# A revised hand-written order for windowed attention followed by a gated convolution: the output projection one group behind the value projection, block-sum trees ahead of their transposes, normalisation in its own step, v in 4096-byte rows, w_out earlier

## The chip, the cores and the metric

The kernel runs on one core of one Trainium2 chip. A core has a matrix engine (PE in the profile; its weight loads are shown as PEld), a vector engine (DVE), a scalar engine (ACT), a general engine (POOL), and a queue engine (SP) that issues the transfers between HBM and the on-chip memory. Each engine works through its own instructions in the order in which they were written, and waits on semaphores for the others. The metric is the device time of one execution in microseconds; lower is better.

## The reference

Inputs are q, k and v of shape (4 batches, 8 heads, 768 positions, 64 dims), and the weights w_val (512 x 512), conv_w (5 x 512) and w_out (512 x 512). What is computed, cut to the core:

```
k_sum = k.reshape(B, H, 24, 32, D).max(axis=3)
v_sum = v.reshape(B, H, 24, 32, D).mean(axis=3)
scores = concat([where(|i-j| < 16, q k^T / 8, -1e9), q k_sum^T / 8 + log(32)])
a      = softmax(scores)
x      = a @ concat([v, v_sum])            # heads side by side: (B, 768, 512)
gate   = sigmoid(causal 5-tap depthwise convolution of x with conv_w)
out    = (gate * (x @ w_val)) @ w_out
```

Each query so sees a window of 31 neighbours and the 24 block summaries of its head.

## The kernel before

**Tiles.** A *unit* (b, th, hp) is a third of a batch's positions (256, four query tiles of 64) for four heads (two pairs of heads, pr). There are 24 units, numbered in order; two units (hp = 0 and 1) make a *group* of 256 positions with all 512 channels, and there are 12 groups (g). Three groups are a batch.

**What one unit goes through.**
- mm_s (line 310): scores on PE into a PSUM tile with one buffer; snorm (line 327): eight DVE instructions that scale, add the mask and take the row minimum of the negated scores.
- exps (line 341): eight exponentials on ACT with their row sums.
- norm (lines 349, 350, 353): two small DVE instructions make the reciprocal ri of the sums; two POOL multiplications apply it to p.
- tp (line 366): two times four PE transposes of p; pcopy (line 370): ACT copies them to SBUF as pts.
- mm_x (line 386): 32 matmuls of pts with v. Besides the window's rows, the v tile holds the batch's block sums, put there by fill_vs (line 187).
- xout (lines 401 to 404): ACT writes x rounded (xh) and in full (xf); POOL takes the difference, xl.
- ginit, taps (lines 416, 427, 431): the convolution, five taps for each of two pairs. The first tap is ACT's in groups below ACT_TAP_G and DVE's from there on; the other four are DVE's.
- gate (line 439): tanh on ACT.

**What one group goes through.** val (line 456) for each half of the channels (cp): 24 matmuls on xh and xl. val_ev (lines 466 to 468): gf = (gate + 1) * val on DVE, its rounded form gh on ACT, the difference gl on POOL. out (line 480) for each half of the positions (si): 12 matmuls on gh and gl of the whole group; out_ev (lines 487, 488): a copy on ACT and the store. Group 0 uses unsplit weights in val. w_val and w_out arrive as 64-bit words; conv_w (lines 200 to 203) turns a quarter of one into float32 with an ACT and two DVE instructions, split_w (lines 240, 241) makes the rounded part on ACT and the rest on POOL. The raw quarters of w_out lie in the buffers of xh and xl, and the staged float32 quarters of w_out have two buffers.

**Per batch.** load_k, load_vT and prep_k (lines 119, 129; DVE: block maxima into the k tile), prep_v (line 140; POOL: block sums as a tree of five adds) and prep_vs (lines 175, 177; PE transposes of the four sums, ACT copy), followed by fill_vs. LOAD_K, PREP_K and PREP_V say how many steps before the batch's first unit these stand.

**The order** is written out by hand, and the program keeps it on each engine. After a prologue for units 0 to 3 comes step(s) for s from 4 to 25 (line 531). A step holds different stages of three units: scores and exponentials of unit s, transposes of unit s-1, mm_x, xout and convolution of unit s-2. Two places in a step, at its start and between the two transposes of unit s-1, call proj(), which takes the next entry from a queue of projections. queue_proj adds val, val, out, out of a group at the end of the step in which the group's second x and gate were made, an odd step. So the step after it runs the two val and the next one the two out. norm(s-1) stands at the start of step s.

Of the kernel before, what the change touches and what calls it, by code (L numbers as in the profile page):

```python
# [35 lines left out]
KALLOC = OFF_A + 2 * STEP * (NT // 2 + 1)  # L36
NK = 5
HALO = NK - 1
REBIAS = 2.0 ** ((127 - 1023) // 8)
NHP = NPR // 2  # L40
NP = 2 * TPU
ACT_TAP_G = 5
LOADS = "k0 q0 m k1 q1 n0 i k2 q2 n1 k3 q3 n2 n3 v0 c Q w0 w1 w2 w3 v1 o0 o1 o2 o3"
LOAD_K = (-4, -3, -2, -1)
PREP_K = (-2, -1, -1, 0)
PREP_V = (-3, -2, -1, 0)


@with_exitstack
def tile_attention_then_gated_conv(  # L50
# [56 lines left out]
    def load_v(g):  # L107
        b, th = divmod(g, NTH)
        t = ld.tile([KW, TPU, DM], F32, tag="v", name=f"v_{g}")
        pieces = ((0, WIN), (OFF_O, OFF_B), (OFF_N, KW)) if g > 1 else ((0, KW),)  # L110
        for r0, r1 in pieces:
            nc.sync.dma_start(t[r0:r1], vw[b, th, r0:r1])
        vtile[g] = t

    def prep_k(b, pr):
# [230 lines left out]
    def norm(u):  # L346
        s = st[u]
        ri = wk.tile([P, NP], F32, tag="ri", name=f"ri_{u}", bufs=4)
        nc.vector.tensor_scalar(ri, s["rs"], 1e-9, None, ALU.add)
        nc.vector.reciprocal(ri, ri)  # L350
        for r in range(2):
            w = slice(TPU * r, TPU * r + TPU)
            nc.gpsimd.tensor_tensor(  # L353
                s["p"][:, w],
                s["p"][:, w],
                ri[:, w].unsqueeze(2).broadcast_to([P, TPU, KW]),
                ALU.mult,
            )
# [49 lines left out]
    def ginit(u):  # L408
        b, th, hp = units[u]
        g = b * NTH + th  # L410
        s = st[u]
        xp = s["xp"]
        gt = s["gt"] = ps_g.tile([P, 2, SG], F32, tag="g", name=f"g_{u}")
        if g < ACT_TAP_G:
            for r in range(2):
                nc.scalar.activation(
                    gt[:, r], xp[:, r], AF.Copy, scale=cwt[:, 2 * hp + r, NK - 1 : NK]
                )

    def taps(u):  # L420
        b, th, hp = units[u]
        g = b * NTH + th
        gt, x = st[u]["gt"], group(g)["xf"]
        for r in range(2):
            pr = 2 * hp + r
            if g >= ACT_TAP_G:
                nc.vector.tensor_scalar(  # L427
                    gt[:, r], x[:, pr, HALO:], cwt[:, pr, NK - 1 : NK], None, ALU.mult
                )
            for o in range(NK - 1):  # L430
                nc.vector.scalar_tensor_tensor(  # L431
                    gt[:, r], x[:, pr, o : o + SG], cwt[:, pr, o : o + 1], gt[:, r],
                    ALU.mult, ALU.add,
                )
# [58 lines left out]
    def proj():  # L493
        if not queue:
            return lambda: None
        mm, ev, g, i = queue.pop(0)
        pp = mm(g, i)
        return lambda: ev(g, i, pp)

    def queue_proj(g):  # L500
        queue.extend((val_mm, val_ev, g, cp) for cp in range(NHP))
        queue.extend((out_mm, out_ev, g, si) for si in range(SG // P))

    def early_loads(s):
        g, hp = divmod(s, NHP)
        if hp == 0 and 1 <= g < NG - 1:
            load_q(g + 1)
        for b in range(1, B):
            for i in range(NPR):
                if s - b * NTH * NHP == LOAD_K[i]:  # L510
                    load_k(b, i)
                    load_vT(b, i)

    def late_loads(s):
        g, hp = divmod(s, NHP)
        for b in range(1, B):
            w = s - b * NTH * NHP
            for i in range(NPR):
                if w == PREP_K[i]:
                    prep_k(b, i)  # L520
                if w == PREP_V[i]:
                    prep_v(b, i)
            if w == 0:
                prep_vs(b)
                fill_vs(b * NTH)
        if hp == NHP - 1 and 1 <= g < NG - 1:
            load_v(g + 1)
            if (g + 1) % NTH:
                fill_vs(g + 1)

    def step(s, late=lambda: None):
        if s < NU:
            early_loads(s)
        if 4 <= s - 1 < NU:
            norm(s - 1)
        ev = proj()
        if s - 2 < NU:
            mm_x(s - 2)
        ev()
        if s - 2 < NU:  # L540
            xout(s - 2)
            ginit(s - 2)
        if s < NU:
            mm_s(s, 0)
            mm_s(s, 1)
            snorm(s, 0)
            snorm(s, 1)
        if s - 1 < NU:
            tp(s - 1, 0)
        if s < NU:  # L550
            exps(s, 0)
        if s - 1 < NU:
            pcopy(s - 1, 0)
        if s < NU:
            exps(s, 1)
        if s - 2 < NU:
            taps(s - 2)
        ev = proj()
        if s - 1 < NU:
            tp(s - 1, 1)  # L560
            pcopy(s - 1, 1)
        ev()
        if s - 2 < NU:
            gate(s - 2)
            if units[s - 2][2] == NHP - 1 and s > 3:
                queue_proj((s - 2) // NHP)
        late()
        if s < NU:
            late_loads(s)

    prep_k(0, 0)
# [37 lines left out]
    mm_s(2, 1)
    snorm(2, 0)  # L610
    snorm(2, 1)
    mm_x(1)
    xout(1)
    conv_w("wv", 1)
    split_w("wv", 0)
    conv_w("wv", 2)
    exps(2, 0)
    split_w("wv", 1)
    conv_w("wv", 3)
    exps(2, 1)  # L620
    early_loads(2)
    mm_s(3, 0)
    mm_s(3, 1)
    ppv = [val_mm(0, 0)]
    taps(0)
    gate(0)
    ginit(1)
    norm(2)
    snorm(3, 0)
    snorm(3, 1)  # L630
    exps(3, 0)
    tp(2, 0)
    pcopy(2, 0)
    val_ev(0, 0, ppv[0])
    exps(3, 1)
    split_w("wv", 2)
    ppv.append(val_mm(0, 1))
    taps(1)
    gate(1)
    tp(2, 1)  # L640
    pcopy(2, 1)
    early_loads(3)
    norm(3)
    val_ev(0, 1, ppv[1])
    split_w("wv", 3)
    conv_w("wo", 0)
    split_w("wo", 0)
    late_loads(3)

    def late4():  # L650
        for k in range(1, 4):
            conv_w("wo", k)
            split_w("wo", k)
        queue.extend((out_mm, out_ev, 0, si) for si in range(SG // P))

    step(4, late4)
    for s in range(5, NU + 2):
        step(s)
    while queue:
        proj()()  # L660
# [6 lines left out]
def _layout(q, k, v, moe_w_val, moe_conv_w, moe_w_out):  # L667
    f = np.float32
    qT = q.reshape(B, NPR, 2, NTH, SG, D).transpose(0, 3, 2, 5, 1, 4)
    qT = qT.reshape(B, NTH, 2 * D, NPR, SG)  # L670
    kt = k.reshape(B, NPR, 2, S, D).transpose(0, 1, 2, 4, 3).reshape(B, NPR, 2 * D, S)
    kT = np.zeros((B, NPR, 2 * D, KTOT), f)
    for t in range(NT):
        c = OFF_O + STEP * t
        kT[..., c : c + QT] = kt[..., t * QT : (t + 1) * QT]
    vT = v.reshape(B, NPR, 2, S, D).transpose(0, 1, 2, 4, 3).reshape(B, NPR, 2 * D, S)
    vn = np.zeros((B, S + 2 * WIN, DM), f)
    vn[:, WIN : WIN + S] = v.transpose(0, 2, 1, 3).reshape(B, S, DM)
    vw = np.zeros((B, NTH, KW, TPU, DM), f)
    for t in range(NT):  # L680
        for r0, r1, s0 in ((0, WIN, 0), (OFF_O, OFF_B, WIN), (OFF_N, KW, WIN + QT)):
            n0 = t * QT + s0
            vw[:, t // TPU, r0:r1, t % TPU] = vn[:, n0 : n0 + r1 - r0]
    cw = moe_conv_w.reshape(NK, NPR, 2 * D).transpose(2, 1, 0).reshape(2 * D, NPR * NK)

    def words(a):
        a = np.ascontiguousarray(a)
        return a.view(np.int64) if a.dtype == np.float64 else a

    loc = np.full(KW, -1)  # L690
    loc[:WIN] = np.arange(WIN)
    loc[OFF_O:OFF_B] = WIN + np.arange(QT)
    loc[OFF_N:] = WIN + QT + np.arange(WIN)
    qi = np.arange(2 * D)[:, None] % QT
    second = np.arange(2 * D)[:, None] >= QT
    maskc = np.zeros((2 * D, 3, KW), f)
    for mv in range(3):
        lo = np.where((mv == 0) & ~second, WIN, 0)
        hi = np.where((mv == 2) & second, WIN + QT, QT + 2 * WIN)
        ok = (loc > qi) & (loc < qi + 2 * WIN) & (loc >= lo) & (loc < hi)  # L700
        m = np.where(ok, 0.0, -1.0e9 * math.sqrt(D))
        m = np.where(loc[None, :] < 0, math.log(BLK) * math.sqrt(D), m)
# [29 lines left out]
```

## Time and profile before

| what | value |
|---|---|
| median of 3 runs | 338.2 us (337.65 to 339.1) |
| the profiled execution | 336.31 us |
| its span, first to last instruction | 334.5 us |
| instructions in it | 7354 |
| mean granted TensorE clock | 0.901 |
| read from HBM, written | 34.71 MB, 6.29 MB |

Columns of the views that follow: a line of the timeline has start in us, duration in us, engine, line, operation, what is written and read, the number of instructions merged, and in brackets the idle time of the engine before it with what ended it. A line of the waits has the waiting engine and line, what it waited for, the total in us, the number of times and the longest. A line of the groups has, behind the first bar, busy time in us and mean ns of one instruction, and behind the second the idle time before them with its releaser.

### The profile page before, as it was taken

The page shows a single profiled execution, that of the slowest core. Times are in us where ns is not written, and L with a number is a line of the kernel's source. Part 1 is how long each engine was busy: PE and PEld are TensorE (multiplying, and loading weights), DVE is VectorE, ACT ScalarE, POOL GpSimd, SP SyncE. Part 2 cuts the span into 40 slices and gives each one's busy share as a digit, 9 for nine tenths or more (in the row PEclk, how much of TensorE's full clock was granted, in tenths as well). Part 3 has the DMA queues.
Part 4 walks back from the last instruction along what each step waited for, and adds up shares of the span by engine and source line. Part 5 has one row for each costly group of instructions (what it writes and reads, how often), then busy time and mean ns, then how long its engine had stood idle before and what let it go on. Part 6 is the DMA issues. An engine that isn't in the chain of part 4 may idle for free.

```text
span 334.5 us, 7354 instructions
## 1 busy us (share of the span) xinstructions
PE 243.8 (73%) x2660; PEld 203.0 (61%) x2660; DVE 218.5 (65%) x750; ACT 183.7 (55%) x593; POOL 149.2 (45%) x187
## 2 busy tenths in 40 slices
PE   1386672289549979788199599696199599695995
PEld 0264451158438859577179488485179488585784
DVE  3956985759835747978638568688638568286160
ACT  3457577426717858686257377266257377273221
POOL 1331366474561557385624345555624415324221
PEclk9999796569969999999689899799699899799698
DMA  7999994113301674726025707544025106000001
GB/s 244 348 323 259 326 275 140 51 46 113 113 10 48 178 280 123 249 88 189 0 58 147 277 31 194 193 135 127 0 57 150 65 35 152 31 33 0 33 31 63
DMA packets 15138, 43.64 MB, mean 130 GB/s; under 512 B 2478, under 2 KB 3246, under 8 KB 13902
## 3 DMA queue, kind: packets, MB, share of 16 engines
q1 hardware_dynamic: 15102, 43.17, 42.1%
q8 instruction: 21, 0.34, 0.5%
q14 instruction: 15, 0.12, 0.1%
HBM read 34.71 MB, written 6.29 MB: 123 GB/s over the span
## 4 chain that ended last, share of the span: by engine, by line
PE 40%; DVE 28%; POOL 8%; issue 3%; ACT 3%; POOLq 0%; DVEq 0%; ACTq 0%
PE out L480 18%; DVE g L431 17%; PE val L456 8%; PE x L386 6%; PE s L310 5%; DVE sn L327 4%; POOL gl L468 3%; POOL vT L140 3%; PE pt L366 2%; DVE g L427 2%; ACT gh L467 2%; DVE gf L466 2%; POOL p L353 2%; DVE wst L203 1%; DVE ks L119 1%
## 5 line engine op out<-in xcount | busy, mean ns | idle before, releaser
L431 DVE SCALAR_TENSOR_TENSOR g<-xf,cwt,g 128x256 f32<-128x256 f32 x192 | 94.0, 490 | 13.6 <-POOL xf L287 7.1
L480 PE MATMUL out<-wo,gh 128*128 128x512 f32 x192 | 63.7, 468 | 31.2 <-ACT gh L467 22.6
L327 DVE CUSTOM_DVE_ANT_0 sn<-s,mask 128x120 f32<-128x120 f32 x192 | 40.9, 278 | 65.9 <-PE s L310 65.8
L341 ACT ACTIVATE p<-sn,nm 128x120 f32<-128x120 f32 x192 | 73.5, 388 | 10.9 <-DVE nm L327 10.9
L353 POOL TENSOR_TENSOR p<-p,ri 128x480 f32<-128x480 f32 x48 | 46.6, 993 | 54.0 <-DVE ri L350 44.4
L480 PEld LDWEIGHTS out<-wo,gh 128*128 128x128 f32 x192 | 39.4, 220 | 44.9 <-ACT gh L467 26.1
L468 POOL TENSOR_TENSOR gl<-gf,gh 128x512 fp32r<-128x512 f32 x24 | 30.8, 1285 | 57.3 <-ACT gh L467 57.3
L456 PE MATMUL val<-xh,wv 128*128 128x256 f32 x352 | 50.4, 285 | 0.0
L404 POOL TENSOR_TENSOR xl<-xf,xh 128x512 fp32r<-128x512 f32 x22 | 29.0, 1316 | 36.3 <-ACT xf L402 30.8
L456 PEld LDWEIGHTS val<-xh,wv 128*128 128x128 f32 x352 | 44.6, 189 | 0.1
L366 PE MATMUL pt<-ident,p 128*120 128x128 f32 x192 | 31.6, 289 | 16.6 <-POOL p L353 9.6
L341 ACT ACTIVATION_READ_ACCUMULATOR p<-sn,nm 128x1 f32 x192 | 36.8, 191 | 0.0
L366 PEld LDWEIGHTS pt<-ident,p 128*120 128x120 f32 x192 | 21.8, 141 | 23.9 <-POOL p L353 12.3
L487 ACT ACTIVATE ob<-out 128x512 f32<-128x512 f32 x24 | 14.3, 596 | 39.9 <-PE out L480 18.9
L467 ACT CAST gh<-gf 128x512 fp32r<-128x512 f32 x24 | 14.9, 619 | 38.4 <-DVE gf L466 38.4
L310 PE MATMUL s<-k,qbd 64*64 64x120 f32 x768 | 27.5, 281 | 10.8 <-DVE k L129 9.9
L386 PEld LDWEIGHTS x<-pts,v 120*64 120x64 f32 x768 | 28.9, 150 | 9.7 <-issue 5.9
L386 PE MATMUL x<-pts,v 120*64 120x64 f32 x768 | 32.5, 239 | 2.1 <-ACT pts L370 1.1
L370 ACT COPY pts<-pt 120x512 f32<-120x512 f32 x48 | 27.4, 572 | 7.2 <-PE pt L366 7.2
L480 PE MATMUL out<-wo,gl 128*128 128x512 f32 x96 | 31.0, 452 | 0.0
L310 PEld LDWEIGHTS s<-k,qbd 64*64 64x64 f32 x768 | 21.0, 139 | 13.6 <-DVE k L129 8.4
L140 POOL TENSOR_TENSOR vT<-vT 128x384 f32<-128x384 f32 (+3 forms) x48 | 27.1, 565 | 2.8
(48 smaller groups left out, 293.5 us busy)
## 6 DMA issues: line engine op xcount, KB each, us to landing
k<-in_kT_dram SPq DMA_DIRECT2D x16, 478.0 KB
vT<-in_vT_dram SPq DMA_DIRECT2D x16, 384.0 KB
out_dram<-ob SPq DMA_DIRECT2D x24, 256.0 KB
qbd<-in_qT_dram SPq DMA_DIRECT2D x11, 512.0 KB
v<-in_vw_dram SPq DMA_DIRECT2D x10, 512.0 KB
v<-in_vw_dram SPq DMA_DIRECT2D x20, 128.0 KB
raw_wv<-in_wv_dram SPq DMA_DIRECT2D x4, 512.0 KB
raw_wo<-in_wo_dram SPq DMA_DIRECT2D x4, 512.0 KB
```

Source lines behind the costliest of these rows:

```text
L140: nc.gpsimd.tensor_tensor(dst, src[:, :, :n], src[:, :, n : 2 * n], ALU.add)
L310: nc.tensor.matmul(st[u]["sp"][64 * e : 64 * e + 64, h, c * KW : c * KW + KW], qbd[g % NQB][64 * h : 64 * h + 64, pr, i * QT : i * QT + QT ...
L327: nc.vector.tensor_tensor_reduce(s["sn"][:, n, :], s["sp"][:, h, c * KW : c * KW + KW], mask[:, mv, :], -1.0 / math.sqrt(D), 3.0e38, ALU.a ...
L341: nc.scalar.activation(s["p"][:, n, :], s["sn"][:, n, :], AF.Exp, bias=s["nm"][:, n : n + 1], scale=-1.0, accum_out=s["rs"][:, n : n + 1],)
L353: nc.gpsimd.tensor_tensor(s["p"][:, w], s["p"][:, w], ri[:, w].unsqueeze(2).broadcast_to([P, TPU, KW]), ALU.mult,)
L366: nc.tensor.transpose(s["pt"][:KW, i, :], s["p"][:, TPU * r + i, :], ident)
L386: nc.tensor.matmul(dst, v[:, i, c0 : c0 + D], src, start=True, stop=g > 0)
L404: nc.gpsimd.tensor_tensor(G["xl"][:, prs, :], x[:, prs, HALO:], G["xh"][:, prs, :].bitcast(F32), ALU.subtract)
L431: nc.vector.scalar_tensor_tensor(gt[:, r], x[:, pr, o : o + SG], cwt[:, pr, o : o + 1], gt[:, r], ALU.mult, ALU.add,)
L456: nc.tensor.matmul(pp[:, r], w, x, start=(n == 0), stop=(n == len(terms) - 1))
L468: nc.gpsimd.tensor_tensor(G["gl"][:, cos, :], gf, G["gh"][:, cos, :].bitcast(F32), ALU.subtract)
L480: nc.tensor.matmul(pp, x, w, start=(n == 0), stop=(n == len(terms) - 1))
```

## The change

1. **Projections.** queue_proj is called in the middle of the odd step, right after xout and ginit, and not at its end; it adds val(g), out(g-1), val(g), out(g-1). out of the last group is added behind its val. out of group 0 is no longer queued in step 4.
2. **Normalisation.** norm(s) stands in step s, behind taps(s-2), and not at the start of step s+1. gate(s-2) stands ahead of the evacuation of the middle projection.
3. **Next group's tiles.** group(g+1), with its halo copy on POOL, is made right behind queue_proj(g).
4. **Loads and preparation of a batch.** For batches 2 and 3 loads, prep_k and prep_v stand one step earlier (prep_k of the first three pairs: -3, -2, -1; the last one stays in the batch's first step). Batch 1 has its own list.
5. **First tap.** ACT takes both first taps of a unit in groups below 3 (before: below 5), and from there on one of two (before: none).
6. **v.** The layout of v in HBM is cut in two, so that a row is 4096 bytes long (before 8192); each piece is loaded with two transfers.
7. **Prologue.** The conversions of w_val stand earlier, those of the first two quarters of w_out stand ahead of taps(1); the splits of w_out are spread over steps 4 and 5; several parts of units 2 and 3 change places.

The diff, cut to its core:

```diff
+VP = TPU // 2
-ACT_TAP_G = 5
+ACT_TAP_G = 3
-LOAD_K = (-4, -3, -2, -1)
-PREP_K = (-2, -1, -1, 0)
-PREP_V = (-3, -2, -1, 0)
+UPB = NTH * NHP
+LOAD_K = {1: (2, 2, 4, 5)}
+PREP_K = {1: (4, 5, 5, 6)}
+PREP_V = {1: (3, 4, 5, 5)}
+for _b in range(2, B):
+    LOAD_K[_b] = tuple(_b * UPB + w for w in (-5, -4, -3, -2))
+    PREP_K[_b] = tuple(_b * UPB + w for w in (-3, -2, -1, 0))
+    PREP_V[_b] = tuple(_b * UPB + w for w in (-4, -3, -2, -1))
...
         for r0, r1 in pieces:
-            nc.sync.dma_start(t[r0:r1], vw[b, th, r0:r1])
+            for e in range(VP):
+                nc.sync.dma_start(t[r0:r1, 2 * e : 2 * e + 2], vw[b, th, e, r0:r1])
...
-        if g < ACT_TAP_G:
-            for r in range(2):
+        for r in range(2 if g < ACT_TAP_G else 1):
...
-            if g >= ACT_TAP_G:
+            if r and g >= ACT_TAP_G:
...
     def queue_proj(g):
-        queue.extend((val_mm, val_ev, g, cp) for cp in range(NHP))
-        queue.extend((out_mm, out_ev, g, si) for si in range(SG // P))
+        for i in range(2):
+            queue.append((val_mm, val_ev, g, i))
+            queue.append((out_mm, out_ev, g - 1, i))
+        if g == NG - 1:
+            queue.extend((out_mm, out_ev, g, i) for i in range(2))
...
     def step(s, late=lambda: None):
...
-        if 4 <= s - 1 < NU:
-            norm(s - 1)
         ev = proj()
...
             xout(s - 2)
             ginit(s - 2)
+            g, hp = divmod(s - 2, NHP)
+            if hp == NHP - 1:
+                queue_proj(g)
+                if g + 1 < NG:
+                    group(g + 1)
...
             taps(s - 2)
+        if u:
+            norm(s)
         ev = proj()
...
             pcopy(s - 1, 1)
+        if x:
+            gate(s - 2)
         ev()
-        if s - 2 < NU:
-            gate(s - 2)
-            if units[s - 2][2] == NHP - 1 and s > 3:
-                queue_proj((s - 2) // NHP)
         late()
```

The prologue's order after it, from norm(1) on, with the lines that differ marked by what they hold now:

```
norm(1); conv_cw(); conv_w("wv", 0); tp(1, 0); pcopy(1, 0); conv_w("wv", 1)
mm_x(0); xout(0); tp(1, 1); pcopy(1, 1); ginit(0)
mm_s(2); snorm(2); conv_w("wv", 2); exps(2, 0); mm_x(1); conv_w("wv", 3); xout(1); exps(2, 1)
group(1); early_loads(2); mm_s(3); snorm(3); norm(2); exps(3)
val_mm(0, 0); val_mm(0, 1); split_w("wv", 0); split_w("wv", 1); taps(0); gate(0); ginit(1); norm(3)
tp(2, 0); pcopy(2, 0); val_ev(0, 0); conv_w("wo", 0); conv_w("wo", 1); taps(1)
tp(2, 1); pcopy(2, 1); gate(1); early_loads(3); split_w("wv", 2); val_ev(0, 1); split_w("wv", 3); late_loads(3)
step 4, then split_w("wo", 0), split_w("wo", 1), conv_w("wo", 2), conv_w("wo", 3)
step 5, then split_w("wo", 2), split_w("wo", 3)
```

More of the change, by code (lines that the diff above doesn't have):

```diff
@@ L413, in ginit @@
         gt = s["gt"] = ps_g.tile([P, 2, SG], F32, tag="g", name=f"g_{u}")
-        if g < ACT_TAP_G:
-            for r in range(2):
-                nc.scalar.activation(
-                    gt[:, r], xp[:, r], AF.Copy, scale=cwt[:, 2 * hp + r, NK - 1 : NK]
-                )
+        for r in range(2 if g < ACT_TAP_G else 1):
+            nc.scalar.activation(
+                gt[:, r], xp[:, r], AF.Copy, scale=cwt[:, 2 * hp + r, NK - 1 : NK]
+            )
     def taps(u):
@@ L509, in early_loads @@
             for i in range(NPR):
-                if s - b * NTH * NHP == LOAD_K[i]:
+                if s == LOAD_K[b][i]:
                     load_k(b, i)
@@ L516, in late_loads @@
         for b in range(1, B):
-            w = s - b * NTH * NHP
             for i in range(NPR):
-                if w == PREP_K[i]:
+                if s == PREP_K[b][i]:
                     prep_k(b, i)
-                if w == PREP_V[i]:
+                if s == PREP_V[b][i]:
                     prep_v(b, i)
-            if w == 0:
+            if s == b * UPB:
                 prep_vs(b)
@@ L531, in step @@
     def step(s, late=lambda: None):
-        if s < NU:
+        u, t, x = s < NU, s - 1 < NU, s - 2 < NU
+        if u:
             early_loads(s)
-        if 4 <= s - 1 < NU:
-            norm(s - 1)
         ev = proj()
-        if s - 2 < NU:
+        if x:
             mm_x(s - 2)
         ev()
-        if s - 2 < NU:
+        if x:
             xout(s - 2)
             ginit(s - 2)
-        if s < NU:
+            g, hp = divmod(s - 2, NHP)
[3 more added lines that the diff above has]
+                    group(g + 1)
+        if u:
             mm_s(s, 0)
@@ L547, in step @@
             snorm(s, 1)
-        if s - 1 < NU:
+        if t:
             tp(s - 1, 0)
-        if s < NU:
+        if u:
             exps(s, 0)
-        if s - 1 < NU:
+        if t:
             pcopy(s - 1, 0)
-        if s < NU:
+        if u:
             exps(s, 1)
-        if s - 2 < NU:
+        if x:
             taps(s - 2)
+        if u:
+            norm(s)
         ev = proj()
-        if s - 1 < NU:
+        if t:
             tp(s - 1, 1)
             pcopy(s - 1, 1)
-        ev()
-        if s - 2 < NU:
-            gate(s - 2)
-            if units[s - 2][2] == NHP - 1 and s > 3:
-                queue_proj((s - 2) // NHP)
+        if x:
+            gate(s - 2)
+        ev()
         late()
-        if s < NU:
+        if u:
             late_loads(s)
@@ L599, in tile_attention_then_gated_conv @@
     conv_cw()
+    conv_w("wv", 0)
     tp(1, 0)
     pcopy(1, 0)
+    conv_w("wv", 1)
     mm_x(0)
+    xout(0)
     tp(1, 1)
     pcopy(1, 1)
-    xout(0)
     ginit(0)
-    conv_w("wv", 0)
     mm_s(2, 0)
@@ L611, in tile_attention_then_gated_conv @@
     snorm(2, 1)
[L612 to L615, printed above, removed]
     conv_w("wv", 2)
     exps(2, 0)
-    split_w("wv", 1)
+    mm_x(1)
     conv_w("wv", 3)
+    xout(1)
     exps(2, 1)
+    group(1)
     early_loads(2)
@@ L623, in tile_attention_then_gated_conv @@
     mm_s(3, 1)
-    ppv = [val_mm(0, 0)]
+    snorm(3, 0)
+    snorm(3, 1)
+    norm(2)
+    exps(3, 0)
+    exps(3, 1)
+    ppv = [val_mm(0, 0), val_mm(0, 1)]
+    split_w("wv", 0)
+    split_w("wv", 1)
     taps(0)
@@ L627, in tile_attention_then_gated_conv @@
     ginit(1)
[L628 to L631, printed above, removed]
+    norm(3)
     tp(2, 0)
@@ L634, in tile_attention_then_gated_conv, with late5 @@
     val_ev(0, 0, ppv[0])
-    exps(3, 1)
-    split_w("wv", 2)
-    ppv.append(val_mm(0, 1))
+    conv_w("wo", 0)
+    conv_w("wo", 1)
     taps(1)
-    gate(1)
     tp(2, 1)
     pcopy(2, 1)
+    gate(1)
     early_loads(3)
-    norm(3)
+    split_w("wv", 2)
     val_ev(0, 1, ppv[1])
     split_w("wv", 3)
-    conv_w("wo", 0)
-    split_w("wo", 0)
     late_loads(3)
     def late4():
-        for k in range(1, 4):
+        for k in range(2):
+            split_w("wo", k)
+        for k in range(2, 4):
             conv_w("wo", k)
+    def late5():
+        for k in range(2, 4):
             split_w("wo", k)
-        queue.extend((out_mm, out_ev, 0, si) for si in range(SG // P))
     step(4, late4)
-    for s in range(5, NU + 2):
+    step(5, late5)
+    for s in range(6, NU + 2):
         step(s)
@@ L678, in _layout @@
     vn[:, WIN : WIN + S] = v.transpose(0, 2, 1, 3).reshape(B, S, DM)
-    vw = np.zeros((B, NTH, KW, TPU, DM), f)
+    vw = np.zeros((B, NTH, VP, KW, 2, DM), f)
     for t in range(NT):
+        i = t % TPU
         for r0, r1, s0 in ((0, WIN, 0), (OFF_O, OFF_B, WIN), (OFF_N, KW, WIN + QT)):
             n0 = t * QT + s0
-            vw[:, t // TPU, r0:r1, t % TPU] = vn[:, n0 : n0 + r1 - r0]
+            vw[:, t // TPU, i // 2, r0:r1, i % 2] = vn[:, n0 : n0 + r1 - r0]
     cw = moe_conv_w.reshape(NK, NPR, 2 * D).transpose(2, 1, 0).reshape(2 * D, NPR * NK)
```

## Prediction

> **What bounds the kernel now.** I read the page's busy shares first, then the table of waits, then the timeline of the steady steps engine by engine, and last the stalls at the batch edges and in the prologue. By "step s" I mean one call of step(s); its place in the trace is the start of its 32 matmuls x<-pts,v, which belong to unit s-2. "+t" counts from there.
>
> ```profile
> PE 243.8 (73%) x2660; PEld 203.0 (61%) x2660; DVE 218.5 (65%) x750; ACT 183.7 (55%) x593; POOL 149.2 (45%) x187
> ```
>
> No engine is full, so order and waits decide, not work. In the table of waits:
>
> ```profile
> PE vsp L175 <- POOL vsT L140: 23.3, 3, 8.2
> PE out L480 <- ACT gh L467: 22.6, 8, 3.5
> PE out L480 <- ACT wo L240: 6.3, 3, 5.5
> POOL xl L404 <- ACT sc_wo L200: 5.5, 1, 5.5
> ```
>
> PE loses 46 us in two places that come back: at each batch's start, where the transposes of the block sums wait for POOL's tree of adds, and in every second step, where out waits for gh of its own group. The timeline of PE, steps 7 and 8 (start, duration, engine, line, what):
>
> ```profile
> 101.51 1.15 PE L386 MATMUL x<-pts,v 120*64 120x64 f32 x32
> ...
> 103.57 0.65 PE L366 MATMUL pt<-ident,p 128*120 128x128 f32 x4
> ...
> 103.98 2.11 PE L480 MATMUL out<-wo,gh 128*128 128x512 f32 x8
> ...
> 106.87 0.60 PE L366 MATMUL pt<-ident,p 128*120 128x128 f32 x4
> ...
> 107.22 1.18 PE L456 MATMUL val<-xh,wv 128*128 128x256 f32 x8
> ...
> 110.21 1.15 PE L386 MATMUL x<-pts,v 120*64 120x64 f32 x32
> ...
> 112.68 1.18 PE L456 MATMUL val<-xh,wv 128*128 128x256 f32 x8
> ...
> 113.70 0.63 PE L456 MATMUL val<-xl,wv 128*128 128x256 f32 x4
> ...
> 119.49 1.20 PE L480 MATMUL out<-wo,gh 128*128 128x512 f32 x4 [2.32 <-ACT gh L467]
> ...
> 121.55 1.15 PE L386 MATMUL x<-pts,v 120*64 120x64 f32 x32
> ```
>
> Step 7 has no wait: 8.70 us, made of x and s 2.06, first transposes 0.41, one projection 2.89, second transposes 0.35, the next projection 2.99. That is PE's floor. Step 8 takes 11.34, because out needs gh. What the other engines do in step 8:
>
> ```profile
> 112.41 0.28 DVE L327 CUSTOM_DVE_ANT_0 sn<-s,mask 128x120 f32<-128x120 f32 x1 [1.40 <-PE s L310]
> ...
> 114.04 4.16 DVE L431 SCALAR_TENSOR_TENSOR g<-xf,cwt,g 128x256 f32<-128x256 f32 x8
> ...
> 118.11 0.68 DVE L466 SCALAR_TENSOR_TENSOR gf<-gt,val 128x512 f32<-128x512 f32 x1
> ...
> 118.90 0.20 DVE L350 RECIPROCAL ri<-ri 128x8 f32<-128x8 f32 x1
> ...
> 119.51 1.29 POOL L468 TENSOR_TENSOR gl<-gf,gh 128x512 fp32r<-128x512 f32 x1 [5.07 <-ACT gh L467]
> ...
> 120.76 1.94 POOL L353 TENSOR_TENSOR p<-p,ri 128x480 f32<-128x480 f32 x2
> ...
> 123.23 0.59 ACT L402 COPY xf<-x 128x512 f32<-128x512 f32 x1
> ...
> 123.90 1.29 POOL L404 TENSOR_TENSOR xl<-xf,xh 128x512 fp32r<-128x512 f32 x1 [1.20 <-ACT xf L402]
> ...
> 125.15 2.52 POOL L140 TENSOR_TENSOR vT<-vT 128x384 f32<-128x384 f32 x4
> ```
>
> DVE does eight sn, eight taps and gf in one row; gf comes last at +7.90, gh follows, and only then PE goes on. Longer idle also costs the clock, and the batch edges cost most (PE timeline again):
>
> ```profile
> 165.93 0.39 PE L175 MATMUL vsp<-ident,vsT 128*24 128x128 f32 x1 [8.16 <-POOL vsT L140]
> ...
> 179.08 1.15 PE L386 MATMUL x<-pts,v 120*64 120x64 f32 x32
> ...
> 189.47 2.07 PE L480 MATMUL out<-wo,gh 128*128 128x512 f32 x4 [3.48 <-ACT gh L467]
> ...
> 193.08 1.15 PE L386 MATMUL x<-pts,v 120*64 120x64 f32 x32
> ...
> 254.24 1.15 PE L386 MATMUL x<-pts,v 120*64 120x64 f32 x32
> ...
> 313.52 1.98 PE L386 MATMUL x<-pts,v 120*64 120x64 f32 x32
> ```
>
> After 3.48 us of idle time the same four matmuls take 2.07 instead of 1.20, and the way from there to x is 3.61 (189.47 to 193.08) against 2.06 (119.49 to 121.55). So an idle time of that size costs 1.55 more, up to 2.4 where x is slow too (1.98 against 1.15).
>
> **The change, part by part.**
>
> *out one group behind val.* Each step now has one out at its start and one val in its middle. gh and gl of out are then older than a step: the 22.6 us go. What is late next is val0, which stands in the middle of the odd step in which xl of its own group is made. I follow an even step and the odd one after it, from x of the even step: sn at +2.20 and taps at +3.83 (rows above), eight taps to +7.90. From group 3 on one first tap is DVE's:
>
> ```profile
> 222.22 0.49 DVE L427 TENSOR_SCALAR g<-xf,cwt 128x256 f32<-128x256 f32 x1
> ...
> 92.75 2.11 DVE L129 COPY k<-ks 128x84 f32<-128x84 f32 x2
> ...
> 81.72 0.31 DVE L129 COPY k<-ks 128x84 f32<-128x84 f32 x2
> ```
>
> With its gap it adds 0.52: +8.45. norm now stands here: two ri instructions of 0.2 and the hand-over, 0.6 together: +9.05. POOL then does p 1.94 (+11.0), gl 1.29 (+12.3), and in the next step xl 1.29: +13.55. xf has been there since 8.70 + 2.3, so POOL's queue sets this. PE has done val0's eight matmuls on xh by 8.70 + 2.47 + 1.02 = +12.2 and idles 1.4. It needs 1.97 for the rest of val0 (2.99 - 1.02), 0.35 for transposes and 2.89 for out: the pair takes 18.8, where PE alone would take 17.4 and the trace has 20.0 (101.51 to 121.55) and later 22.7.
>
> *norm in its own step.* It takes ri and p out of the start of the next step: p's first half is done at +10, the transposes want it at 8.70 + 2.06. DVE's ri waits for the last exp, which ends about when the taps do; behind it stand gf and prep_k. I cost it at nothing, covered by the taps; without that cover it would be at most 1.5 per step.
>
> *Trees steps ahead.* vsp stands at the end of steps 6, 12 and 18 with its sums ready a step before: 23.3 us of waits go, 0.9 per batch of PE work stays. But POOL does a tree (2.52 and a small last add, 2.7) at the end of steps 8, 10, 14 and 16, straight before xl of the odd step: those four pairs take 18.8 + 2.7 = 21.5, PE idles 4.1 in each, and by the 3.48 row the clock drops: 1.55 to 2.4, I take 1.8 each, 7.2 in all. Trees at the end of odd steps meet val1, which needs no new xl. prep_k moves a step ahead too, except the last one of a batch, which still stands one step before the scores that read it: DVE ends it near +12, the scores want it near +11.2, 1.2 lost. So the pair at the batch edge is 17.4 + 0.9 + 1.2 = 19.5.
>
> A prep_k's two copies take 0.31 while POOL is idle and 2.11 beside POOL's work. The Trainium skill, GPSIMD Engine Reference, section 1 (Specifications), says that GpSimd shares its SBUF interfaces with VectorE and that VectorE instructions in a 2-port mode or with two SBUF inputs contend there. The two rows agree. In the new order p and gl stand on POOL just when prep_k runs, so the long form is the rule. My pairs use the long form already and find DVE's slack (it ends gf near +9.6, next sn is wanted at +10.9) nearly enough; where it isn't, that is a rival.
>
> *Steps 7 to 24.* Step 7: 9.0. Steps 8 to 13: 21.5 + 21.5 + 19.5 = 62.5; steps 14 to 19 the same; steps 20 to 24: 18.8 + 18.8 + 8.7 = 46.3; clock 7.2. Sum 187.5, against 212.0 (101.51 to 313.52).
>
> *v in 4096-byte rows.* SP's queue:
>
> ```profile
> 110.01 1.64 SPq L112 DMA_DIRECT2D v<-in_vw_dram  x3
> ...
> 111.69 3.33 SPq L187 DMA_DIRECT2D v<-vs  x4
> ```
>
> Three issues become six: 1.64 more per group, ten groups. Behind them stand the fills of the same tile, q, and out's store. x reads the tile three steps later, over 26 us; so 0, and 16 if nothing covered it. What smaller rows do to the transfers themselves the trace can't show. In the prologue v0 and v1 are 1.97 MB, some 7 us of transfer; a tenth of it either way is 0.7. I take 0.
>
> *ACT_TAP_G.* Groups 3 and 4: DVE +0.52 a unit; groups 5 to 11: DVE -0.52, all counted in the pair. ACT's side hides in ACT's idle 45%.
>
> *w_out sooner, prologue.* The rows for it, from the groups by line and DVE's timeline:
>
> ```profile
> L203 DVE SCALAR_TENSOR_TENSOR wst<-sc_wo,wst 128x512 uint32<-128x512 uint32 x4 | 5.2, 1312 | 2.8 <-ACT sc_wo L200 2.7
> ...
> L241 POOL TENSOR_TENSOR wo<-wst,wo 128x512 fp32r<-128x512 f32 x4 | 5.2, 1312 | 2.5 <-ACT wo L240 2.5
> ...
> L202 DVE TENSOR_SCALAR wst<-raw_wo 128x512 uint32<-128x512 uint32 x4 | 3.3, 820 | 0.0
> ```
> ```profile
> 46.76 0.65 DVE L466 SCALAR_TENSOR_TENSOR gf<-gt,val 128x512 f32<-128x512 f32 x1
> ```
>
> Two w_out conversions (4.3) go ahead of that gf, DVE's waits for sc_wv and a ri leave (about 3): I put gf at 47.4 to 48. From there the chain is: sn 1.65, xf and the first tap on ACT (to 51), taps 4.2 (55), ri 0.4, p 1.94 (57.4), first split 1.31 (58.7), DVE's two conversions 4.3 and a prep_k 2.1 (65.1), sn and taps 5.8 and ri 0.6 (71.5), p, gl and two splits 5.9 (77.3), the rest of out0 at half clock 2.2, x of step 6 at 79.5; x and s at half clock 2.6, transposes, val1, vsp, out1 7.9 and small gaps: step 7 at 90.5, against 101.51. The 11 us come from vsp's wait of the first batch (7) and from the waits for wo. Without the long DVE forms it would be 86, with all of them and waits for landing 97.
>
> *Tail.* One projection more is left after step 25's x. x, xh, xf, xl end at 3.65; val0's rest 1.97; then out, val, out, out, out without a wait (gf needs the taps at 7.1 and is ready at 8.4) 14.7: 20.3.
>
> ```profile
> 330.91 0.60 ACT L487 ACTIVATE ob<-out 128x512 f32<-128x512 f32 x1 [2.21 <-PE out L480]
> ```
>
> From there to the span's end, 334.5, are 3.7: tail 24.0, against 20.98: 3 lost.
>
> *Sum.* 90.5 + 187.5 + 24.0 = 302.0 of span; the profiled run took 336.31, 1.8 more than its span: 303.8. Against its median of 338.2 that run is 1.9 low, so on the scale of the median 306.
>
> **Rivals.**
> 1. PE becomes the bound: trees and p slip in without holding xl. Eighteen steps of 8.7 and two vsp of 0.9 are 158.4, 29 less: 277 is the floor; with only the four tree waits and their clock gone it is 288. For: PE is the fullest engine. Against: POOL's chain is in every pair.
> 2. DVE and POOL hold each other: by the rule above every copy and conversion takes its long form and nothing hides it. Twelve prep_k by 1.8 are 21.6: up to 328, half of it 317. For: the 2.11 row. Against: DVE's slack of 1.3 a step.
> 3. The change doesn't shorten the pairs (20.0 and 22.7 stay, since sn, taps, ri and p still follow each other) and takes only the vsp waits: two of 8.2 and the prologue's 11, less the tail's 3: 314.
> 4. Slower. PE's idle in every odd step, 1.4 us before xl, is already enough to drop the clock. Then val's rest, transposes and out run at 3.61/2.06 = 1.75 of their time: 5.2 by 0.75 is 3.9 in nine odd steps, and x, s and the transposes after them 2 more: 53 instead of 7.2, about 350. It decides from about 4.2 per odd step on. Against: 2.32 us of idle left 1.20 unharmed.
>
> **How the numbers follow.** Forecast 306, its own range 299 to 313: 0.45. Rival 1, 277 to 299: 0.20. Rivals 2 and 3, 313 to 330: 0.27. Within 0.5% of before (about what a measurement here can tell from no change): 0.03. Rival 4: 0.05. So faster 0.92, same 0.03, slower 0.05. The range takes the upper half of rival 1 and most of 2 and 3, with the prologue's 86 to 97 in it: 291 to 322.
>
> **What would show it.** In the changed profile: no wait of out for gh and of vsp for vsT (each under 2 us in total); the waits of PE for POOL xl new, near 1.4 in ordinary odd steps and 4 in steps 9, 11, 15 and 17; pairs of 18.8 and 21.5; step 7's x near 90; 24 us after the last x. Wrong would be pairs of 17.4 (rival 1), DVE copies with waits of sn behind them (rival 2), or a clock well under 0.9 (rival 4).

## The result, and the profile after

The changed kernel takes 299.64 us (median of 4 runs, 298.97 to 300.61) against 337.92: a ratio of 0.887, 95% interval 0.883 to 0.890. Its profiled execution took 299.31 us, with a span of 297.5. In some runs of a kernel the granted clock is lower and the time some per cent longer, and comparisons leave these out (below, two runs of norm_back and one of own_group_end, whose profile comes from that run). The page of the changed kernel, first and second part (busy us and shares; the granted clock in 40 slices):

```profile
PE 235.7 (79%) x2660; PEld 202.0 (68%) x2660; DVE 211.6 (71%) x740; ACT 185.7 (62%) x603; POOL 148.6 (50%) x187
...
PEclk9999996687599997998999997997999999999999
```

PE does the same 2660 matmuls in 8 us less busy time, because its clock drops less often: the mean is 0.935 against 0.901, and busy time multiplied by mean clock is the same before and after (219.7 and 220.4). The waits of PE, in the table of waits of the changed kernel:

```profile
PE val L462 <- POOL xl L411: 22.5, 8, 5.7
PE pt L373 <- ACT pts L377: 11.6, 3, 10.3
PE s L317 <- DVE k L136: 8.5, 5, 2.6
PE s L317 <- DMA qbd<-in_qT_dram: 5.4, 1, 5.4
PE pt L373 <- POOL p L360: 3.4, 2, 2.5
PE out L486 <- POOL wo L248: 2.3, 1, 2.3
PE out L486 <- ACT wo L247: 2.3, 1, 2.3
```

out for gh and vsp for vsT are gone, both in full. val for xl is new, as large as the wait of out was: 5.7 us in step 5, four times 3.5 in the pairs with a tree, and 0.8 each in steps 21, 23 and 25. Where it sits shows in PE's timeline, at x of steps 7 and 8, of the even steps 10, 12, 14, 22 and 24, and of step 25, with two of val's waits among them:

```profile
89.74 1.15 PE L393 MATMUL x<-pts,v 120*64 120x64 f32 x32
...
99.58 1.15 PE L393 MATMUL x<-pts,v 120*64 120x64 f32 x32
...
115.72 0.80 PE L462 MATMUL val<-xl,wv 128*128 128x256 f32 x2 [3.54 <-POOL xl L411]
...
122.12 1.15 PE L393 MATMUL x<-pts,v 120*64 120x64 f32 x32
...
144.92 1.15 PE L393 MATMUL x<-pts,v 120*64 120x64 f32 x32
...
164.38 1.15 PE L393 MATMUL x<-pts,v 120*64 120x64 f32 x32
...
242.63 0.50 PE L462 MATMUL val<-xl,wv 128*128 128x256 f32 x2 [0.82 <-POOL xl L411]
...
247.71 1.15 PE L393 MATMUL x<-pts,v 120*64 120x64 f32 x32
...
266.27 1.15 PE L393 MATMUL x<-pts,v 120*64 120x64 f32 x32
...
274.04 1.15 PE L393 MATMUL x<-pts,v 120*64 120x64 f32 x32
```

A pair (an even step and the odd one behind it) takes 22.5 and 22.8 us where a tree runs at the end of the even step (99.58, 122.12, 144.92), 19.5 at the batch's edge (to 164.38) and 18.6 where there is no tree (247.71 to 266.27). The wait is 3.5 with a tree and 0.8 without. POOL's timeline in the first of these pairs says why:

```profile
110.42 1.29 POOL L474 TENSOR_TENSOR gl<-gf,gh 128x512 fp32r<-128x512 f32 x1
111.67 2.47 POOL L147 TENSOR_TENSOR vT<-vT 128x384 f32<-128x384 f32 x4
114.22 0.22 POOL L147 TENSOR_TENSOR vsT<-vT 128x24 f32<-128x24 f32 x1
114.41 1.26 POOL L411 TENSOR_TENSOR xl<-xf,xh 128x512 fp32r<-128x512 f32 x1
```

The four stand back to back, xl last, and xl is the one PE wants first.

### The profile page after: what moved, and what is told of

Same layout as the page of the kernel before. It is cut to its first block, busy times and chain, and to the rows that moved or that the text cites. A ratio compares the mean times of both kernels' runs of the same rounds, so it can differ in the third digit from the quotient of the medians.

```text
span 297.5 us, 7371 instructions
## 1 busy us (share of the span) xinstructions
PE 235.7 (79%) x2660; PEld 202.0 (68%) x2660; DVE 211.6 (71%) x740; ACT 185.7 (62%) x603; POOL 148.6 (50%) x187
## 4 chain that ended last, share of the span: by engine, by line
DVE 34%; PE 33%; POOL 16%; DMA 8%; ACT 4%; issue 4%; SPq 0%; POOLq 0%; DVEq 0%; ACTq 0%
DVE g L437 18%; PE out L486 14%; PE val L462 10%; DVE sn L334 6%; POOL p L360 5%; DMA raw_wv<-in_wv_dram 4%; PE x L393 4%; PE s L317 4%; POOL gl L474 3%; POOL vT L147 3%; POOL xl L411 3%; DVE k L136 2%; PE pt L373 2%; DMA k<-in_kT_dram 2%; DMA qbd<-in_qT_dram 2%
## 5 line engine op out<-in xcount | busy, mean ns | idle before, releaser
L486 PE MATMUL out<-wo,gh 128*128 128x512 f32 x192 | 53.6, 420 | 4.6 <-POOL wo L248 2.3
L462 PE MATMUL val<-xh,wv 128*128 128x256 f32 x352 | 54.1, 298 | 0.2
L462 PE MATMUL val<-xl,wv 128*128 128x256 f32 x176 | 32.8, 304 | 22.5 <-POOL xl L411 22.5
L462 PEld LDWEIGHTS val<-xh,wv 128*128 128x128 f32 x352 | 47.7, 200 | 0.8 <-ACT xh L408 0.6
L486 PEld LDWEIGHTS out<-wo,gh 128*128 128x128 f32 x192 | 36.1, 199 | 13.0 <-POOL wo L248 3.4
L373 PE MATMUL pt<-ident,p 128*120 128x128 f32 x192 | 32.8, 298 | 15.0 <-ACT pts L377 11.6
L462 PEld LDWEIGHTS val<-xl,wv 128*128 128x128 f32 x176 | 27.0, 208 | 24.1 <-POOL xl L411 24.1
L445 ACT ACTIVATE gt<-g 128x512 f32<-128x512 f32 x24 | 14.4, 599 | 36.5 <-DVE g L437 36.5
L373 PEld LDWEIGHTS pt<-ident,p 128*120 128x120 f32 x192 | 22.6, 146 | 19.8 <-POOL vT L147 11.1
L393 PEld LDWEIGHTS x<-pts,v 120*64 120x64 f32 x768 | 27.5, 143 | 10.2 <-issue 7.2
L393 PE MATMUL x<-pts,v 120*64 120x64 f32 x768 | 30.9, 231 | 1.5 <-ACT g L422 0.9
```

The lines of the kernel that those rows point to most:

```text
L373: nc.tensor.transpose(s["pt"][:KW, i, :], s["p"][:, TPU * r + i, :], ident)
L393: nc.tensor.matmul(dst, v[:, i, c0 : c0 + D], src, start=True, stop=g > 0)
L462: nc.tensor.matmul(pp[:, r], w, x, start=(n == 0), stop=(n == len(terms) - 1))
L486: nc.tensor.matmul(pp, x, w, start=(n == 0), stop=(n == len(terms) - 1))
```

## The experiments

Times are medians of four runs. Kernels were timed beside the kernel before on their own chip, so they are compared with the changed kernel by their ratio to before; times of before were 337.1 to 337.9 in all of them. Where an expectation gives theory A no other content, it is that of the prediction: POOL works in order, and what stands ahead of xl there sets a pair.

**1. own_group: out behind val of its own group, without the lag.** The queue is still filled in the middle of the odd step; out of group 0 runs at the end of step 5.

```diff
-        for i in range(2):
-            queue.append((val_mm, val_ev, g, i))
-            queue.append((out_mm, out_ev, g - 1, i))
...
+        queue.extend((val_mm, val_ev, g, cp) for cp in range(NHP))
+        queue.extend((out_mm, out_ev, g, si) for si in range(SG // P))
```

> The changed kernel, with out back right behind val of its own group (val, val, out, out), but the queue still filled in the middle of the odd step; out of group 0 is run at the end of step 5. Theory A (what took away out's wait is that val starts half a step earlier, so val1 stands at the start of the even step and its gf goes ahead of DVE's sn and taps; the lag of a group adds nothing): out waits for gh under 3 us in total, pairs of steps stay at 18.5 to 22.8, the tail is one projection shorter, 294 to 300 us. Theory B (the lag itself is what pays): out waits for gh again, 2.3 to 3.5 us in each of some ten pairs, 320 us or more.

290.49 us, ratio 0.861 (0.858 to 0.864): 9 us *faster* than the changed kernel, more than expected. out waits for gl 0.4 us in all and for gh 0.2. With the queue filled this early, the lag of one group is not needed for that. The timeline of its steps 10 and 11 (x at 125.99 and 134.69), DVE, PE and POOL:

```profile
126.20 0.69 DVE L472 SCALAR_TENSOR_TENSOR gf<-gt,val 128x512 f32<-128x512 f32 x1 [1.42 <-POOL gl L474]
...
128.46 2.13 PE L486 MATMUL out<-wo,gh 128*128 128x512 f32 x8
...
134.98 1.93 POOL L360 TENSOR_TENSOR p<-p,ri 128x480 f32<-128x480 f32 x2 [3.50 <-DVE ri L357]
...
136.87 2.49 POOL L147 TENSOR_TENSOR vT<-vT 128x384 f32<-128x384 f32 x4
...
139.62 1.27 POOL L411 TENSOR_TENSOR xl<-xf,xh 128x512 fp32r<-128x512 f32 x1
```

gf of val1 is made ahead of sn and taps, so gh is there when out starts, 2.3 us later. And no gl stands between p and xl: pairs without a tree fall from 18.5 to 17.6, and at the batch edges PE's wait for prep_k (1.4 in the changed kernel) all but goes. Over steps 7 to 24 this makes 10.4 us, which was not expected. The other effects nearly cancel: step 7 starts 6.0 later (95.70 against 89.74), since out of group 0 now stands before it, and the tail is 4.8 shorter.

**2. own_group_end: run 1 with the queue filled at the end of the odd step again.**

```diff
-                queue_proj(g)
...
         ev()
+        if x and units[s - 2][2] == NHP - 1:
+            queue_proj((s - 2) // NHP)
         late()
```

> As own_group, and the queue filled at the end of the odd step as in the kernel before: val, val in the even step, out, out in the odd one. Both theories: out waits for gh, since gf stands behind taps and ri: gh at about +10.2 of the even step, wanted at about +6.9, so 3.3 us in ten pairs and some 1.5 for the clock in each, but no wait for xl: pairs near 22, about 305 to 312 us. If it is within 1% of the changed kernel, the order of projections brought nothing at all and the gain came from the trees and the prologue.

Ratio 0.961 (0.957 to 0.966), some 324 us: 34 us slower than own_group by the place of this one call, more than was expected. The wait is back in the table of waits of this kernel:

```profile
PE out L486 <- ACT gh L473: 27.9, 11, 3.2
PE pt L373 <- ACT pts L377: 25.0, 6, 10.1
```

The second row was not expected. Of it, 10.1 stand in step 4 as in the changed kernel and 9.2 in step 5; the rest, 1.4 in each of steps 10, 12, 16 and 18, is PE waiting for ACT's copies of the transposes, which stand behind the late gh in ACT's order. That the one holds the other is read from the order, and no run takes it apart. Nor was the lag tried with the queue filled at the end, so whether the lag alone would also have taken away out's wait stays open. With out in its old place and the changed kernel's trees and prologue, the time is still 13 us under before.

**3. norm_back: norm(s-1) at the start of step s.**

```diff
+        if 4 <= s - 1 < NU:
+            norm(s - 1)
         ev = proj()
...
-        if u:
-            norm(s)
```

> The changed kernel with norm(s-1) back at the start of step s. Theory A (POOL's queue sets the pair): ri comes behind gf and prep_k, p's first half about 1.2 us or more after the transposes want it, gl goes ahead of p and xl behind it: 0.5 to 1.5 us a step in 18 steps, 308 to 325 us, with PE waiting for POOL p some 10 to 25 us in total. Rival (norm's place is hidden either way): within 1% of the changed kernel.

302.34 and 303.51 us in the two runs that can be compared: 3 to 4 us slower than the changed kernel (ratio about 0.899 against 0.887, with no interval of its own). That is less than theory A expected and slightly more than the rival. The table of waits shows a trade, not a loss added:

```profile
PE pt L373 <- POOL p L360: 34.8, 18, 6.9
PE val L462 <- POOL xl L411: 2.3, 5, 0.9
```

In the changed kernel these rows had 3.4 and 22.5. PE waits for p before it waits for xl, and by then xl is there. Moving norm alone moves most of the wait along POOL's queue.

**4. trees_back: loads, prep_k and prep_v where they were before.**

```diff
+for _b in range(1, B):
+    LOAD_K[_b] = tuple(_b * UPB + w for w in (-4, -3, -2, -1))
+    PREP_K[_b] = tuple(_b * UPB + w for w in (-2, -1, -1, 0))
+    PREP_V[_b] = tuple(_b * UPB + w for w in (-3, -2, -1, 0))
```

> The changed kernel with loads, prep_k and prep_v of all batches back at the steps of the kernel before. Theory A: vsp waits for the last tree, 6 us and 1.5 of clock in each of three batches, but one of two tree waits of xl per batch goes (3 to 4 us each): net 4 to 6 us per batch, 307 to 316 us. Rival (the trees' place is worth the full 23 us of waits seen before): 320 us or more.

319.4 us, ratio 0.947 (0.943 to 0.950): 20 us slower, at the rival's edge. The waits of this kernel:

```profile
PE vsp L180 <- POOL vsT L145: 25.3, 3, 8.6
PE val L460 <- POOL xl L409: 17.1, 8, 5.8
```

The vsp wait comes back at 8.4 us each, not the 6 that were expected, and xl's wait falls by 5 only. So about half of the change's 38 us is the new place of the loads, prep_k and the trees, which this run moves together. Half of these 20 us comes ahead of step 7, which starts at 99.42 here.

**5. v_rows_8k: rows of 8192 bytes and half the transfers.**

```diff
-            for e in range(VP):
-                nc.sync.dma_start(t[r0:r1, 2 * e : 2 * e + 2], vw[b, th, e, r0:r1])
+            nc.sync.dma_start(t[r0:r1], vw[b, th, r0:r1])
```

> The changed kernel with v in 8192-byte rows and half as many transfers, as before. My account: 0, within 1 us of the changed kernel. Rival (shorter rows land sooner, which the start of the kernel, where transfers run all the time, would show): 2 to 5 us slower, with step 4 later than 40.

301.26 us, ratio 0.892 (0.887 to 0.897) against 0.887 (0.883 to 0.890): no difference that can be told. The doubled issues show in SP's queue, 3.22 us for six against 1.68 for three, and hardly anything waits for v either way: PE's weight loads 1.1 us in all, against 0.7 with 8192-byte rows.

**6. wout_back: w_out where it was.**

```diff
-    conv_w("wo", 0)
-    conv_w("wo", 1)
     taps(1)
...
+    conv_w("wo", 0)
+    split_w("wo", 0)
     late_loads(3)
...
+        for k in range(1, 4):
+            conv_w("wo", k)
+            split_w("wo", k)
```

> The changed kernel with the conversions and splits of w_out where they stood before (one quarter at the end of the prologue, three at the end of step 4). My account: out0 of group 0 stands in step 6, so the splits are done in time; xl of step 4 waits for the second raw quarter to be converted, and DVE does three conversions in a row beside POOL's splits: step 7's x 3 to 8 us later than 89.7, 302 to 308 us. Rival (in the new order the place of w_out doesn't matter, since nothing reads it before step 6): within 1 us of the changed kernel.

295.47 us, ratio 0.875 (0.869 to 0.880): 4 us *faster*, the opposite of what I expected. xl of step 4 does wait for the raw quarter, 2.9 us (the first row, POOL's timeline of wout_back), and holds p behind it, for which PE waits 2.2 at 58.65. Yet step 5 is the shorter one, 22.7 against 25.6, and step 4 too, 13.0 against 14.4:

```profile
55.69 1.78 POOL L411 TENSOR_TENSOR xl<-xf,xh 128x512 fp32r<-128x512 f32 x1 [2.87 <-ACT sc_wo L207]
...
64.24 1.27 POOL L248 TENSOR_TENSOR wo<-wst,wo 128x512 fp32r<-128x512 f32 x1 [1.81 <-ACT wo L247]
```

All four quarters are split by 65.5 here. In the changed kernel two splits are left for the end of step 5, behind p and gl on POOL (the first row, POOL's timeline), and PE's out0 of group 0 stands and waits (its PE timeline):

```profile
75.18 2.50 POOL L248 TENSOR_TENSOR wo<-wst,wo 128x512 fp32r<-128x512 f32 x2
...
73.67 0.50 PE L486 MATMUL out<-wo,gh 128*128 128x512 f32 x1 [2.31 <-ACT wo L247]
...
76.50 2.03 PE L486 MATMUL out<-wo,gh 128*128 128x512 f32 x3 [2.32 <-POOL wo L248]
...
80.16 1.57 PE L393 MATMUL x<-pts,v 120*64 120x64 f32 x32
```

Step 6 begins at 80.16 there and at 76.02 in wout_back. "Sooner" held for the conversions of the first two quarters only: the first split comes at 58.31 in the changed kernel and at 48.81 here, and the last one ends 12 us later (77.7 against 65.5).

**7. trees_behind_xl: each tree in the next step, behind xl.**

```diff
-                if s == PREP_V[b][i]:
-                    prep_v(b, i)
...
+            for b in range(1, B):
+                for i in range(NPR):
+                    if s - 1 == PREP_V[b][i]:
+                        prep_v(b, i)
```

> The changed kernel with each tree moved from the end of its step to the next step, right behind xl, where POOL waits for ri. Theory A (PE's waits of 3.6 us for xl in steps 9, 11, 15, 17 are POOL's queue: the tree stands in front of xl): these four waits fall to the 0.8 of the other pairs and the slow clock behind them goes, four pairs from 22.7 to 18.5, so 16 us less: 281 to 286 us, no wait of vsp. Rival (the pairs are bound by DVE, with prep_k in just these steps): pairs stay over 21, less than 5 us won.

287.96 us, ratio 0.853 (0.847 to 0.858): 11 to 12 us faster instead of 14 to 18. The four pairs did fall to 18.5 and 18.6, 16 us together. 5 were given back: vsp waits again for the last tree, step 7 starts at 92.4 instead of 89.7, and the pairs at the batch edges take 20.8 instead of 19.5.

**8. both_behind_xl: gl behind xl as well.** gl goes into a list that is emptied behind the next step's xl.

```diff
+            while owed:
+                owed.pop(0)()
```

> As trees_behind_xl, and gl too goes behind the next step's xl (out reads it a step or more later). Theory A: xl then waits for p alone; the last 0.8 us of PE's wait per pair go and pairs reach PE's own 17.4: nine by about 1, so 273 to 279 us, with PE's clock at 1.0 from step 8 on. Rival (DVE or ACT is the next bound right behind, or gl comes too late for out): no gain over trees_behind_xl beyond 1%.

282.52 us, ratio 0.837 (0.832 to 0.841): another 5 us faster, but above the 273 to 279 of theory A. Pairs are at 18.0, not PE's 17.4: 0.3 of the wait for xl is left in each. The same last tree costs at the edges (PE timeline):

```profile
88.83 0.39 PE L182 MATMUL vsp<-ident,vsT 128*24 128x128 f32 x1 [2.45 <-POOL vsT L147]
...
145.76 0.28 PE L182 MATMUL vsp<-ident,vsT 128*24 128x128 f32 x1 [1.36 <-POOL vsT L147]
```

**9. own_trees: the edits of 1 and 7 together.**

> own_group (out right behind val of its own group, queue filled in the middle of the odd step) and trees_behind_xl together. Theory A (two separate savings in POOL's queue: own_group takes gl of val1 out from between p and xl, trees_behind_xl takes the tree out): they add, the four pairs of 20.1 to 21.7 fall to about 17.6 like the others, 13.5 us less than own_group's 290.5, some given back at the batch edges where the last tree now ends later: 276 to 281 us. Rival (both remove the same wait): no better than trees_behind_xl, 288.

296.1 us, ratio 0.875 (0.870 to 0.880): slower than either. Neither theory had this. Four of its six pairs inside a batch (from steps 8, 14, 20 and 22) take 17.6 as hoped, but its even steps 10 and 16 take 11.3 instead of 8.7, steps 12 and 18 take 14.6 where own_group has 9.3 and 9.1, and step 6 takes 14.1 instead of 9.2. DVE, ACT and PE in step 10 (x at 127.55), and PE at the end of step 12:

```profile
128.88 1.92 DVE L136 COPY k<-ks 128x84 f32<-128x84 f32 x2
...
130.73 0.67 DVE L472 SCALAR_TENSOR_TENSOR gf<-gt,val 128x512 f32<-128x512 f32 x1
131.43 0.62 ACT L473 CAST gh<-gf 128x512 fp32r<-128x512 f32 x1 [2.79 <-DVE gf L472]
...
132.10 1.20 PE L486 MATMUL out<-wo,gh 128*128 128x512 f32 x4 [0.89 <-ACT gh L473]
...
135.42 0.66 PE L373 MATMUL pt<-ident,p 128*120 128x128 f32 x4 [1.18 <-ACT pts L377]
...
157.69 0.32 PE L182 MATMUL vsp<-ident,vsT 128*24 128x128 f32 x1 [1.08 <-POOL vsT L147]
157.73 3.66 PE L486 MATMUL out<-wo,gh 128*128 128x512 f32 x8
```

In this order gf of val1 stands behind the odd step's prep_k, whose copies take their long form beside POOL. While PE waited for xl in the odd step, prep_k was done in time. With that wait gone gf is late, gh with it, and on ACT gh stands ahead of xh, the exponentials and the copies of the transposes. In steps 10 and 16 the lost tree wait has become a wait for DVE. Steps 12 and 18 have the same waits for gh and pts, and on top of them vsp waits for the last tree, which this order makes late as run 7 does; behind these waits out's eight matmuls take 3.66 instead of 2.13. Step 6 has the vsp waits alone (0.7 and 2.4), and its out is nearly as slow (3.52). Against own_group these five steps lose 21 us, of which steps 6, 12 and 18 make up 16.

**10. both_wout: 8 with w_out of 6.**

> both_behind_xl with w_out at its old place. The prologue is apart from the steady steps, so the 4 us that the old place won add: 278 to 280 us against 282.5, with step 7's x some 4 us earlier. If it is not faster than 282.5, the 4 us were not the prologue's.

279.86 us, ratio 0.827 (0.823 to 0.832): 3 us less, about what was expected, with step 7 at 90.17 instead of 93.22.

**11. own_trees_wout: 9 with earlier trees and w_out of 6.** Out of group 0 runs at the end of step 5; the trees of batches 2 and 3 stand in the middle of the step in which the changed kernel has them at its end.

```diff
+                if b == 1 and s == PREP_V[b][i]:
+                    prep_v(b, i)
...
-            for b in range(1, B):
+            for b in range(2, B):
...
-                    if s - 1 == PREP_V[b][i]:
+                    if s == PREP_V[b][i]:
```

> own_trees with the trees of batches 2 and 3 one step earlier still (in the middle of the step in which the changed kernel has them at the end), those of batch 1 as in the changed kernel, and w_out converted and split at its old place, with out of group 0 at the end of step 5. Theory A: no wait of vsp, pairs near 17.6 everywhere but at the edges (19), prologue some 4 us shorter: 268 to 275 us. Rival (PE's clock or DVE becomes the bound): not faster than 278.

280.84 us, ratio 0.830 (0.826 to 0.833): the rival's value. vsp waits for nothing now, and steps 6, 12 and 18 fall to 9.2, 11.8 and 11.8. Steps 10 and 16 are still at 11.3, with the same waits for gh and pts as in run 9, and steps 12 and 18 keep them too.

**12. both_wout_early: 10 with the trees of 11.**

```diff
+            for b in range(2, B):
+                for i in range(NPR):
+                    if s == PREP_V[b][i]:
+                        prep_v(b, i)
```

> both_wout with the trees of batches 2 and 3 one step earlier (in the middle of the step in which the changed kernel has them at the end) and those of batch 1 at the ends of their steps as in the changed kernel. Account: in both_wout vsp still waits for the last tree, 2.0 us in step 6 and 1.4 at each later batch edge, and batch 1's trees stand in front of p in step 6; that goes: step 7's x from 90.2 to about 85 to 87, edges from 19.5 to 18, so 272 to 276 us against 279.9. Rival (vsp's wait is covered by prep_k and the scores behind it): within 1% of both_wout.

272.28 us (271.96 to 272.5), ratio 0.807 (0.803 to 0.811): the fastest, 27 us under the changed kernel. Its page, busy and clock, and two rows of its waits:

```profile
PE 229.4 (85%) x2660; PEld 197.1 (73%) x2660; DVE 206.9 (77%) x740; ACT 186.2 (69%) x603; POOL 150.2 (56%) x187
...
PEclk9999998575699999999999999999999999999999
```
```profile
PE val L462 <- POOL xl L411: 5.9, 8, 3.2
PE val L462 <- ACT xh L408: 4.6, 1, 4.6
```

Step 7 starts at 85.2, 5.0 sooner than in both_wout, vsp waits for nothing, the clock stays up from step 6 to the end, and pairs and edges lie between 18.0 and 18.5. The wait for xh and 3.2 of that for xl stand in step 5.

## Why the prediction was right, and where it was not

| term | predicted | measured |
|---|---|---|
| x of step 7 | 90.5 | 89.74 |
| step 7 | 9.0 | 9.84 |
| pairs with a tree, with clock | 21.5 + 1.8 | 22.5, 22.8, 22.6, 22.8 |
| pairs at the batch edge | 19.5 | 19.5, 19.5 |
| pairs without a tree | 18.8 | 18.5, 18.6 |
| step 24 | 8.7 | 7.8 |
| steps 7 to 24 | 187.5 | 184.3 |
| tail | 24.0 | 23.5 |
| span | 302.0 | 297.5 |

*The pair.* Following one chain over two steps (sn, taps, ri, p, gl, xl, val) gave the length of a pair without a tree to 0.3 us. The wait behind it was 0.8 and 3.5 instead of 1.4 and 4.1, in part because two of val0's first four matmuls on xl, 0.4 us, read the xl of the group's first unit and run ahead of the wait. Runs 7 and 8 show that the chain is the cause: with the tree moved from ahead of xl the wait falls from 3.5 to 0.8 or 0.9, and with gl moved too to 0.3.

*The clock.* Priced at 1.8 per tree wait. From val's restart to the next x it is 6.4 to 6.7 with a tree (115.72 to 122.12 is 6.40) and 5.08 without (242.63 to 247.71): 1.3 to 1.6. The 0.8 wait cost no clock, so rival 4 did not come. But the length of one wait does not settle the price, as the prediction's reading of 2.32 and 3.48 us took it to. In the kernel before, two of the waits of 3.48 left the four matmuls behind them at 1.20 and 1.21 (at 212.20 and 287.36) and only the next four were slow, 1.78 and 1.84 instead of 1.10. In own_group, after waits of 2.39 and 2.36 us, the two matmuls that follow took 0.80 at 119.51 and 0.50 at 140.94, and val's next eight 1.91 and 1.10.

*Steps 24 and 7* were mis-sized: there is no unit 24, so step 24 has no scores, 1.0 less, and in step 7 the scores wait 0.9 for prep_k.

*The cause of out's lost wait* is where the prediction's story was incomplete, though its number was good. It put the 22.6 us down to gh and gl being older than a step, by the lag. Runs 1 and 2 show that the queue's earlier filling does it without the lag and is worth 34 in that order, and that beside it the lag costs 9; what the lag would do alone was not run. The "one projection more" of the tail, which the prediction charged with 3, is no net loss: without the lag the tail is 4.8 shorter and step 7 6.0 later. The 9 us lie in the steps between.

*w_out.* The prediction counted the vsp wait of the first batch and the waits for wo as the 11 us saved at step 7. They came (101.51 to 89.74), but 10.3 of them in step 6 alone (19.91 to 9.58), where vsp had waited 7.0; step 6 itself starts only 1.4 sooner than before (80.16 against 81.60). Run 4 gives 9.7 back with batch 1's loads, prep_k and trees, and run 6 shows that w_out's new place costs 4.6 at step 7. The other changes of the prologue no run here takes apart.

*norm* at nothing, at most 1.5 a step: run 3 gives 3 to 4 us in all, with the wait moved from p to xl. *Trees*: 23 us of waits were to go, and run 4, which moves the loads and prep_k as well, lost 20. *v rows* at 0: run 5 agrees within its interval. ACT_TAP_G was not tried by itself.

*Rival 2* (the long form of DVE's copies): from step 6 on, five of nine prep_k have copies of 1.9 in the changed kernel and four of 0.3 to 0.5. DVE's slack hides them but for the last one of each batch, for which the scores wait 0.9 to 1.4. Runs 9 and 11 show the rival where the slack is gone: 2.6 us in each of steps 10 and 16.

*Rival 3* (the pairs don't get shorter) held for four of the six pairs inside a batch. The two that begin with steps 8 and 10 went from 20.1 and 21.0 to 22.5 and 22.8, and those of steps 14 and 16 stayed at 22.6 to 22.8: there the wait for gh was traded for one for xl. The 37 us of span came from the start of step 7 (11.8), the two pairs at the batch edges (18.6), the two last pairs (8.4) and step 24 (6.1), less some 8 in the first two pairs, step 7 and the tail.

## What to carry to other kernels

On an engine that works in order, ask of every instruction who waits for it and how soon, and put what is wanted a step later behind what is wanted now: a tree and a subtraction moved by a few lines were worth 17 us here without any work removed. Before a buffered lag is put into a pipeline, try to start the producer half a step earlier; here that removed the same wait without the lag, and the lag beside it cost 9 us. When a wait goes, look at what was done during it: prep_k of step 9 had been free only as long as PE waited.

## What the runs showed that I had not expected

Two edits that each saved time (9 and 11 us) were together slower than either (296.1 against 290.5 and 288.0). And a call moved by half a step in a list, with no instruction added or taken away, was worth 34 us with out in its old order, in a kernel whose engines each work through a list in order.
